# Retention attention and two feed-forward layers on one core: conversions begun in turn and kept in a PSUM bank, another order of the first loads

## The chip, the cores and the metric

One core of one Trainium2 chip. Time is device microseconds of one launch. The kernel before takes 644.09 us, the median of three runs (643.82 to 646.04).

## The reference

The inputs are q, k, v of shape (2, 8, 768, 64), one decay lam per head, and weights of two feed-forward layers. The weights are float64.

```
per block of 64 tokens, head by head (D[i,j] = lam^(i-j) for i >= j, else 0):
    out   = (q k^T * D) v + (q * lam^(i+1)) state
    state = lam^64 * state + (k * lam^(63-i))^T v
x = out as 1536 tokens x 512
h = x @ w_in                               # 512 x 2048
g = h where h >= 1, 0 where h <= -1, else (h + 1)^2 / 4
x = g @ w_out                              # 2048 x 512
y = ((x @ w_a) * (x @ w_b)) @ w2_out       # 512 x 1536 twice, 1536 x 512
```

## The kernel before, in words

**Attention.** The 1536 tokens are 12 chunks of 128 (6 per batch). `load_chunk` fetches four pieces of 256 KB per chunk (q and k by feature, k and v by token) into 16 buffers, named load. Per chunk, TensorE makes the scores (L149), VectorE multiplies them by the decay table dmask (`att_mask`, L179), GpSimd decays k (`att_kd`, L160) and q (`att_qd`, L171), TensorE sums the state's update (L193) and the output (L220 from the state, L224 from the masked scores). ScalarE casts the output to fp32r (the high part, L236), and VectorE subtracts that from it (the low part, L240). The three 512-token blocks of x hold high and low parts. The tables dmask and tabq are written to DRAM and read back by `tables`, which waits for GpSimd's powers of lam.

**Matrix products.** Each operand is a high and a low fp32r part, and a product is high x high + high x low + low x high: `mm3`, L354, three matmuls of 512 columns for each 128 of the inner dimension. `product_in` is 12 of them. A PSUM tile is one of eight banks, `bank()` hands them out in rotation.

**Weights.** `load_w` fetches one raw tile of 512 KB (128 x 512 float64) into one of four buffers, in the fixed order `order` of 68 tiles. `weight_pieces` is a generator that turns raw tiles into high and low parts, in pieces that `bg` takes between other work. Per tile: `begin` (ScalarE: absolute value of the upper word into hc, L279; the lower word scaled into c, L280), then VectorE clips hc (L292), shifts it into v (L294), joins the sign (L298) and adds c (L307); ScalarE casts the high part (`split_act`, L264), GpSimd subtracts (L265). `begin` of tile n+1 is issued inside tile n, after L298. `done(n)` runs the pieces until n tiles are ready. For the second layer, `strassen_weights` (L329) also forms sums and differences of a pair of tiles, s12 and s34, and splits them.

**Order.** Every engine works through its instructions in the order of the program, which is written out by hand. First the prologue (L514 to L575): tables, chunks 0 to 3, weight tiles 0 and 1, and fillers for TensorE (`warm`). Then the loop (L579 to L607): eight products of the first layer, `h_bank`, each beside the attention of one of the chunks 4 to 11. Then the stages of the first layer (L622 to L635). Then the second layer: six groups, each two calls of `both_banks` (a Strassen-like scheme over two token blocks, the third block by plain products) and three `o_stage`, which sum the output over the groups: in SBUF for blocks 0 and 1, in four banks held in PSUM for block 2 (`held`). All DMA of chunks and weights is issued by SP, in order; a `load_w` whose buffer is still being read holds up what is behind it.

Of the kernel before, what the change touches and what calls it, by code (L numbers as in the profile page):

```python
# [35 lines left out]
def retention_ffn_kernel(ctx: ExitStack, tc: tile.TileContext, lam, att, w1i, w1o, w2ab, w2o, out):  # L36
# [18 lines left out]
    four = deque(const.tile([128, 2, 512], F32R, name=f"four{i}") for i in range(19))  # L55
    two = deque(const.tile([128, 512], F32, name=f"two{i}") for i in range(18))

    banks = deque(ps_p.tile([128, 512], F32, name=f"ps{i}") for i in range(8))

    def bank():  # L60
        banks.rotate(-1)
# [4 lines left out]
    def t2(name):  # L66
        return two.popleft()

    def free2(*tiles):
        two.extend(tiles)  # L70
# [45 lines left out]
    def store_powers():  # L116
        nc.scalar.dma_start(out=raw_ap(CH + 1, [[PITCH, H], [8, 16], [1, 8]]), in_=base)
# [20 lines left out]
    def load_chunk(c, parts=(0, 1, 2, 3)):  # L138
        t = ck.setdefault(c, [None] * 4)
        for i in parts:  # L140
            t[i] = loads.popleft()
            nc.sync.dma_start(out=t[i], in_=att[c, i])
# [25 lines left out]
    def att_qd(c, engine):  # L168
        if c % CPB:
            qd[c] = t2("qd")  # L170
            engine.tensor_tensor(out=qd[c], in0=ck[c][0], in1=tabq.rearrange("p a i -> p (a i)"), op=ALU.mult)  # L171
        loads.append(ck[c][0])
# [83 lines left out]
    def load_w():  # L256
        if todo_loads:
            key = todo_loads.popleft()
            r = raw_p.tile([128, 1024], I32, tag="raw", name="raw")
            nc.sync.dma_start(out=r, in_=srcs[key[0]][key[1]].bitcast(I32))  # L260
            raws[key] = r
# [13 lines left out]
    def begin(key):  # L275

        r = raws[key].rearrange("p (c w) -> p c w", w=2)
        hc, c = t2("hc"), t2("c")
        nc.scalar.activation(out=hc, in_=r[:, :, 1].bitcast(F32), func=ACTF.Abs)  # L279
        nc.scalar.activation(out=c.bitcast(I32), in_=r[:, :, 0].bitcast(U32), func=ACTF.Copy, scale=2.0**-29)  # L280
        return hc, c

    def weight_pieces():

        nxt = begin(order[0])
        for n, key in enumerate(order):
            hc, c = nxt
            high = raws.pop(key).rearrange("p (c w) -> p c w", w=2)[:, :, 1]
            v = t2("v")


            nc.vector.tensor_scalar(out=hc, in0=hc, scalar1=HIGH_MIN, scalar2=HIGH_MAX, op0=ALU.max, op1=ALU.min)  # L292
            hc, v, c = (t.bitcast(I32) for t in (hc, v, c))
            nc.vector.tensor_scalar(  # L294
                out=v, in0=hc, scalar1=3, scalar2=0x3FFFFFFF, op0=ALU.logical_shift_left, op1=ALU.bitwise_and
            )
            yield 0
            nc.vector.scalar_tensor_tensor(  # L298
                out=v, in0=high, scalar=-0x40000000, in1=v, op0=ALU.bitwise_and, op1=ALU.bitwise_or
            )  # L300
            load_w()
            if n + 1 < len(order):
                if order[n + 1] not in raws:
                    load_w()
                nxt = begin(order[n + 1])
            yield 0
            nc.vector.tensor_tensor(out=v, in0=v, in1=c, op=ALU.add)  # L307
            hc, v, c = (t.bitcast(F32) for t in (hc, v, c))
            free2(hc, c)
            w = four.popleft()  # L310
            split_act(v, w[:, 0], w[:, 1])
            wt[key] = w
            if key[0] != "2i":
                free2(v)
            elif key[1] % 2 == 0:
                v_a.append(v)
            else:
                yield 0
                yield from strassen_weights(key[1] // 2, v_a.pop(), v)
            yield 1  # L320
# [88 lines left out]
    def both_banks(ft):  # L409

        wa, wb = wt["2i", 2 * ft], wt["2i", 2 * ft + 1]
        s12, s34 = sw.pop(ft)
        half_w = lambda w, i: [[w[:, a, (2 * i + j) * 128:(2 * i + j + 1) * 128] for a in range(2)] for j in range(2)]
        half_y = lambda nb, i: [[xy[nb][2 * i + j][:, a] for a in range(2)] for j in range(2)]
        half_t = lambda i: [[ts[i, j][:, a] for a in range(2)] for j in range(2)]

        def prod(w, x):
            ps = bank()
            mm3(ps, list(zip(w, x)))
            return ps  # L420

        add = lambda o, x, ps: nc.vector.tensor_tensor(out=o, in0=x, in1=ps, op=ALU.add)  # L422
        s, u, w, b0 = (t2(name) for name in ("s", "u", "w", "b0"))
        nc.scalar.copy(s, prod(half_w(wa, 0), half_y(0, 0)))  # L424
        bg()
        add(u, s, prod(half_w(s12, 1), half_t(2)))
        bg()
        a = t2("a")
        nc.scalar.copy(a, product_in("2i", 2 * ft, 2))
        bg(2)  # L430
        add(s, s, prod(half_w(wa, 1), half_y(0, 1)))
        add(w, u, prod(half_w(s34, 0), half_t(3)))
        bg()
        add(b0, w, prod(half_w(wb, 1), half_t(4)))
        nc.vector.tensor_tensor(out=b0, in0=b0, in1=s, op=ALU.mult)
        give_g(ft, 0, b0)
        pb = product_in("2i", 2 * ft + 1, 2)
        bg(2)
        nc.vector.tensor_tensor(out=a, in0=a, in1=pb, op=ALU.mult)
        give_g(ft, 2, a)  # L440
        pd = prod(half_w(s12, 0), half_t(1))
        add(w, w, pd)
        add(u, u, pd)
        add(u, u, prod(half_w(s34, 1), half_y(1, 1)))
        nc.vector.tensor_tensor(out=u, in0=u, in1=w, op=ALU.mult)
        give_g(ft, 1, u)
        free2(s, w)
        four.extend((s12, s34, wt.pop(("2i", 2 * ft)), wt.pop(("2i", 2 * ft + 1))))
# [34 lines left out]
    def o_bank(g, nb, m, last):  # L483
        fts = range(2 * g, 2 * g + 2)
        r0 = nb * TB + m * 128
        pairs = [([gt[2, f, nb][:, a, m * 128:(m + 1) * 128] for a in range(2)],
                  [wt["2o", f][:, b] for b in range(2)]) for f in fts]
        if nb < NB - 1:
            ps = bank()
            mm3(ps, pairs)  # L490
            o = acc["o", nb, m] = gather(acc.get(("o", nb, m)), ps, g == 0)
            if last:
                nc.sync.dma_start(out=out[r0:r0 + 128], in_=o)
            return
        mm3(held[m], pairs, g == 0, last)
        if last:
            o = t2("o")
            for i, copy, queue in ((0, nc.vector.tensor_copy, nc.sync), (1, nc.scalar.copy, nc.scalar)):
                cols = slice(i * DM // 2, (i + 1) * DM // 2)
                copy(o[:, cols], held[m][:, cols])  # L500
                queue.dma_start(out=out[r0:r0 + 128, cols], in_=o[:, cols])
# [13 lines left out]
    load_chunk(0, (0, 1))  # L515
    load_w()
    load_chunk(0, (2, 3))
    store_powers()
    tables()
    load_chunk(1)  # L520
    load_chunk(2)
    load_chunk(3)
    load_w()
    load_w()
    load_w()
    warm(8)
# [8 lines left out]
    bg(2)  # L535
    att_mask(0)
    low0 = att_out(0)
    att_scores(2)
    att_qd(0, nc.gpsimd)
    att_qd(1, nc.gpsimd)  # L540
    att_kd(1, nc.gpsimd)
    att_mask(1)
    low0()
    att_done(0)
    load_chunk(4, (0, 1, 2))
    add1 = att_state(1)
    add1()
    att_kd(2, nc.gpsimd)
    low1 = att_out(1)
    add2 = att_state(2)  # L550
    att_done(1)
    att_qd(2, nc.vector)
    att_scores(3)
    att_mask(2)
    low1()
    add2()
    att_kd(3, nc.gpsimd)
    low2 = att_out(2)
    att_done(2)
    att_qd(3, nc.gpsimd)  # L560
    add3 = att_state(3)
    att_mask(3)
    low2()
    add3()
    low3 = att_out(3)
    att_done(3)
    load_chunk(4, (3,))
    load_chunk(5)
    att_scores(4)
    bg()  # L570
    low3()
    att_kd(4, nc.gpsimd)
    att_qd(4, nc.gpsimd)
    att_mask(4)
    bg(2)  # L575


    at["limit"] = 8
    for nb in range(2):  # L579
        for j in range(4):  # L580
            c = 4 + 4 * nb + j
            low = []

            def attention():
                if j < 3 and c + 1 < NCHUNK:
                    att_scores(c + 1)

            h_bank(j, nb, attention)
            low = att_out(c)
            add = att_state(c)  # L590
            if j == 3 and c + 1 < NCHUNK:
                att_scores(c + 1)
            att_done(c)
            if c + 2 < NCHUNK:
                load_chunk(c + 2)
            if c + 1 < NCHUNK:
                if j < 3:
                    att_mask(c + 1)
                att_kd(c + 1, nc.gpsimd)
                att_qd(c + 1, nc.gpsimd)  # L600
            low()
            add()
            if j == 3 and c + 1 < NCHUNK:
                att_mask(c + 1)
            bg(3)
        if nb:
            done(8)  # L607
# [28 lines left out]


    groups = FF2 // 256
    for m in range(KT):
        held[m] = banks.popleft()  # L640
    for g in range(groups):
        at["limit"] = 32 + 6 * g + 6
# [58 lines left out]
```

## Time and profile before

| | |
|---|---|
| median of three runs | 644.09 us |
| the profiled execution | 646.91 us, its span 645.1 us |
| TensorE busy | 608.3 us (94%), granted clock 0.971 |
| VectorE busy | 489.1 us (76%) |
| ScalarE busy | 267.0 us (41%) |
| GpSimd busy | 282.4 us (44%) |
| DMA | 52.72 MB, mean 82 GB/s |

PE is TensorE, DVE is VectorE, ACT is ScalarE, POOL is GpSimd, SP issues DMAs. A row of the waits says who sat idle until whose instruction ended; L numbers are lines of the kernel above. The clock is the share of TensorE's full rate that was granted (1.00 is 2.4 GHz, 0.50 is 1.2 GHz). Times in windows and timelines count from the span's start.

### The profile page before, as it was taken

The numbers are of one execution on the slowest core, as the hardware profiler recorded it, in microseconds if no ns is written. First come the engines' busy times: TensorE is split into PE (matmuls) and PEld (weight loads), VectorE is DVE, ScalarE is ACT, GpSimd is POOL, SyncE is SP. The second block draws the span as 40 slices with busy tenths as digits, with TensorE's granted clock in tenths as the row PEclk, the third lists the DMA queues.
The fourth block names the chain that finished last, engine by engine and source line by source line (L and its number), as shares of the span: only waits on it lengthen the run. The fifth ranks groups of instructions, "written<-read, shape, count | busy, mean of one in ns | idle before, by whom it ended". The sixth has DMA issues, their size and how long they took to land. (4 is left out here: it accounts for less than half of the span.)

```text
span 645.1 us, 8349 instructions
## 1 busy us (share of the span) xinstructions
PE 608.3 (94%) x3099; PEld 496.0 (77%) x3100; DVE 489.1 (76%) x681; ACT 267.0 (41%) x473; POOL 282.4 (44%) x217
## 2 busy tenths in 40 slices
PE   6398889999999999999998999999989989989997
PEld 3386678888888888888886888878868878868886
DVE  2169863487775977597869999999969979969653
ACT  1135543366543544265545355534423433424210
POOL 2235662246433543343857455544533443444320
PEclk9689889999999999999999899999989999989999
DMA  5926560022110211022100222212202302300004
GB/s 163 359 90 222 197 198 2 33 99 98 66 66 34 99 65 66 33 90 67 41 1 34 65 99 66 98 33 99 99 0 70 102 26 69 105 23 2 1 17 179
DMA packets 21081, 52.72 MB, mean 82 GB/s; under 512 B 2600, under 2 KB 5168, under 8 KB 21040
## 3 DMA queue, kind: packets, MB, share of 16 engines
q1 hardware_dynamic: 19624, 51.39, 23.3%
q10 hardware_dynamic: 1416, 0.80, 0.5%
q8 instruction: 24, 0.39, 0.2%
q14 instruction: 17, 0.14, 0.1%
HBM read 49.03 MB, written 3.15 MB: 81 GB/s over the span
## 5 line engine op out<-in xcount | busy, mean ns | idle before, releaser
L265 POOL TENSOR_TENSOR four<-two,four 128x512 fp32r<-128x512 f32 x107 | 142.7, 1340 | 238.2 <-ACT four L264 214.0
L354 PE MATMUL ps<-block,four 128*128 128x512 f32 x828 | 200.8, 396 | 5.4 <-POOL block L265 2.3
L354 PEld LDWEIGHTS ps<-block,four 128*128 128x128 f32 x828 | 157.1, 191 | 40.8 <-POOL block L265 3.1
L354 PE MATMUL ps<-four,four 128*128 128x512 f32 x633 | 163.9, 393 | 4.1 <-ACT two L424 4.1
L354 PEld LDWEIGHTS ps<-four,four 128*128 128x128 f32 x633 | 119.6, 189 | 30.7 <-ACT two L424 5.3
L264 ACT CAST four<-two 128x512 fp32r<-128x512 f32 x107 | 66.0, 620 | 137.7 <-DVE two L307 42.9
L265 POOL TENSOR_TENSOR late_four<-two,late_four 128x512 fp32r<-128x512 f32 x46 | 62.6, 1363 | 58.0 <-ACT late_four L264 42.6
L354 PE MATMUL ps<-block,late_four 128*128 128x512 f32 x324 | 77.2, 389 | 0.0
L354 PEld LDWEIGHTS ps<-block,late_four 128*128 128x128 f32 x324 | 60.8, 188 | 12.6
L354 PE MATMUL ps<-four,late_four 128*128 128x512 f32 x243 | 64.9, 393 | 2.0 <-ACT late_two L424 2.0
L354 PE MATMUL ps<-late_four,four 128*128 128x512 f32 x213 | 59.9, 396 | 0.1
L373 ACT ACTIVATE two<-two,half 128x512 f32<-128x512 f32 x42 | 30.4, 723 | 66.1 <-DVE two L372 66.1
L422 DVE TENSOR_TENSOR two<-two,ps 128x512 f32<-128x512 f32 x66 | 44.1, 683 | 15.6 <-PE ps L354 9.6
L372 DVE TENSOR_SCALAR two<-ps 128x512 f32<-128x512 f32 x42 | 28.8, 686 | 35.6 <-PE ps L354 35.5
L354 PEld LDWEIGHTS ps<-four,late_four 128*128 128x128 f32 x243 | 45.9, 189 | 11.9 <-ACT late_two L424 2.4
L458 DVE TENSOR_TENSOR two<-two,ps 128x512 f32<-128x512 f32 x60 | 40.4, 678 | 18.6 <-PE ps L354 18.6
L298 DVE SCALAR_TENSOR_TENSOR two<-raw,two 128x512 int32<-128x512 int32 x56 | 53.1, 949 | 0.4
L264 ACT CAST late_four<-two 128x512 fp32r<-128x512 f32 x46 | 28.5, 622 | 55.6 <-DVE two L307 13.5
L354 PEld LDWEIGHTS ps<-late_four,four 128*128 128x128 f32 x213 | 40.8, 192 | 9.1 <-DVE two L422 0.6
L307 DVE CUSTOM_DVE_ANT_0 two<-two,two 128x1024 uint16<-128x1024 uint16 x51 | 46.1, 905 | 1.8
L279 ACT ACTIVATE two<-raw 128x512 f32<-128x512 f32 x55 | 36.8, 670 | 12.9 <-DMA raw<-in_w1i 12.9
L292 DVE TENSOR_SCALAR two<-two 128x512 f32<-128x512 f32 x55 | 33.3, 606 | 11.5 <-ACT two L279 11.5
(103 smaller groups left out, 649.8 us busy)
## 6 DMA issues: line engine op xcount, KB each, us to landing
load<-in_att SPq DMA_DIRECT2D x48, 256.0 KB, 5.0
raw<-in_w2ab SPq DMA_DIRECT2D x24, 512.0 KB, 3.2
raw<-in_w1i SPq DMA_DIRECT2D x16, 512.0 KB, 3.3
raw<-in_w1o SPq DMA_DIRECT2D x16, 512.0 KB, 3.3
raw<-in_w2o SPq DMA_DIRECT2D x12, 512.0 KB, 3.2
out<-two SPq DMA_DIRECT2D x6, 256.0 KB, 2.0
dmask<-rows SPq DMA_DIRECT2D x2, 256.0 KB, 4.6
out<-late_two SPq DMA_DIRECT2D x2, 256.0 KB, 2.0
```

The source lines that it names most:

```text
L264: nc.scalar.copy(hi, src)
L265: (engine or nc.gpsimd).tensor_tensor(out=lo, in0=src, in1=hi.bitcast(F32), op=ALU.subtract)
L279: nc.scalar.activation(out=hc, in_=r[:, :, 1].bitcast(F32), func=ACTF.Abs)
L292: nc.vector.tensor_scalar(out=hc, in0=hc, scalar1=HIGH_MIN, scalar2=HIGH_MAX, op0=ALU.max, op1=ALU.min)
L298: nc.vector.scalar_tensor_tensor(out=v, in0=high, scalar=-0x40000000, in1=v, op0=ALU.bitwise_and, op1=ALU.bitwise_or)
L307: nc.vector.tensor_tensor(out=v, in0=v, in1=c, op=ALU.add)
L354: nc.tensor.matmul(out=ps, lhsT=l[a], rhs=r[b], start=(start and i == 0 and j == 0), stop=(stop and i == n - 1 and j == 2))
L372: nc.vector.tensor_scalar(out=r, in0=ps, scalar1=-1.0, scalar2=1.0, op0=ALU.max, op1=ALU.min)
L373: nc.scalar.activation(out=r, in_=r, func=ACTF.Square, scale=0.5, bias=half)
L422: add = lambda o, x, ps: nc.vector.tensor_tensor(out=o, in0=x, in1=ps, op=ALU.add)
L458: nc.vector.tensor_tensor(out=total, in0=total, in1=ps, op=ALU.add)
```

## The change

- `begin` of tile n is issued at the head of tile n for tiles 0 to 3, and inside tile n-1 only from tile 4 on.
- The absolute value goes to one PSUM bank of its own, `words`, in place of an SBUF buffer; clip and shift stay there, and L298 reads it. Seven banks rotate in place of eight.
- In the prologue, q and k of chunk 1 are loaded ahead of the tables, weight tile 1 ahead of chunk 3, and chunks 4 to 6 are loaded before the loop, which then fetches chunk c + 3 in place of c + 2. Scores of chunks 2 and 3 are issued after the output of the chunk before. The pieces of tile 1 are spread over chunks 2 to 4.
- In `both_banks` the last sums of a and b stay in the bank of their product (pf, pg), and the product a x b reads them there.
- Of block 2's output, the first 128 rows (m = 0) are no longer held in PSUM but summed in SBUF as those of the other blocks.

```diff
-    banks = deque(ps_p.tile([128, 512], F32, name=f"ps{i}") for i in range(8))
+    banks = deque(ps_p.tile([128, 512], F32, name=f"ps{i}") for i in range(7))
+    words = ps_p.tile([128, 512], F32, name="words")
...
-        hc, c = t2("hc"), t2("c")
-        nc.scalar.activation(out=hc, in_=r[:, :, 1].bitcast(F32), func=ACTF.Abs)
+        c = t2("c")
+        nc.scalar.activation(out=words, in_=r[:, :, 1].bitcast(F32), func=ACTF.Abs)
...
-        nxt = begin(order[0])
+        nxt = None
         for n, key in enumerate(order):
-            hc, c = nxt
+            c = nxt or begin(key)
+            nxt = None
...
-            nc.vector.tensor_scalar(out=hc, in0=hc, scalar1=HIGH_MIN, scalar2=HIGH_MAX, op0=ALU.max, op1=ALU.min)
-            hc, v, c = (t.bitcast(I32) for t in (hc, v, c))
             nc.vector.tensor_scalar(
-                out=v, in0=hc, scalar1=3, scalar2=0x3FFFFFFF, op0=ALU.logical_shift_left, op1=ALU.bitwise_and
+                out=words, in0=words, scalar1=HIGH_MIN, scalar2=HIGH_MAX, op0=ALU.max, op1=ALU.min
+            )
+            word, v, c = (t.bitcast(I32) for t in (words, v, c))
+            nc.vector.tensor_scalar(
+                out=word, in0=word, scalar1=3, scalar2=0x3FFFFFFF, op0=ALU.logical_shift_left, op1=ALU.bitwise_and
             )
             yield 0
             nc.vector.scalar_tensor_tensor(
-                out=v, in0=high, scalar=-0x40000000, in1=v, op0=ALU.bitwise_and, op1=ALU.bitwise_or
+                out=v, in0=high, scalar=-0x40000000, in1=word, op0=ALU.bitwise_and, op1=ALU.bitwise_or
             )
             load_w()
-            if n + 1 < len(order):
+            if 4 <= n + 1 < len(order):
...
-        add(b0, w, prod(half_w(wb, 1), half_t(4)))
-        nc.vector.tensor_tensor(out=b0, in0=b0, in1=s, op=ALU.mult)
+        pf = prod(half_w(wb, 1), half_t(4))
+        add(pf, w, pf)
+        nc.vector.tensor_tensor(out=b0, in0=s, in1=pf, op=ALU.mult)
...
-        add(u, u, prod(half_w(s34, 1), half_y(1, 1)))
-        nc.vector.tensor_tensor(out=u, in0=u, in1=w, op=ALU.mult)
+        pg = prod(half_w(s34, 1), half_y(1, 1))
+        add(pg, u, pg)
+        nc.vector.tensor_tensor(out=u, in0=w, in1=pg, op=ALU.mult)
...
-        if nb < NB - 1:
+        if m not in held or nb < NB - 1:
...
     load_chunk(0, (2, 3))
+    load_chunk(1, (0, 1))
     store_powers()
     tables()
-    load_chunk(1)
+    load_chunk(1, (2, 3))
     load_chunk(2)
+    load_w()
     load_chunk(3)
-    load_w()
     load_w()
     load_w()
...
     low0 = att_out(0)
-    att_scores(2)
     att_qd(0, nc.gpsimd)
+    att_kd(1, nc.gpsimd)
     att_qd(1, nc.gpsimd)
-    att_kd(1, nc.gpsimd)
     att_mask(1)
     low0()
     att_done(0)
-    load_chunk(4, (0, 1, 2))
     add1 = att_state(1)
     add1()
+    low1 = att_out(1)
+    att_done(1)
+    att_scores(2)
     att_kd(2, nc.gpsimd)
-    low1 = att_out(1)
+    att_qd(2, nc.gpsimd)
+    low1()
+    att_mask(2)
     add2 = att_state(2)
-    att_done(1)
-    att_qd(2, nc.vector)
-    att_scores(3)
-    att_mask(2)
-    low1()
     add2()
-    att_kd(3, nc.gpsimd)
     low2 = att_out(2)
     att_done(2)
+    bg(1)
+    load_chunk(4)
+    att_scores(3)
+    low2()
+    att_kd(3, nc.gpsimd)
     att_qd(3, nc.gpsimd)
+    att_mask(3)
     add3 = att_state(3)
-    att_mask(3)
-    low2()
     add3()
     low3 = att_out(3)
     att_done(3)
-    load_chunk(4, (3,))
     load_chunk(5)
+    bg(1)
+    low3()
     att_scores(4)
-    bg()
-    low3()
     att_kd(4, nc.gpsimd)
     att_qd(4, nc.gpsimd)
+    bg(1)
     att_mask(4)
-    bg(2)
+    load_chunk(6)
...
-            if c + 2 < NCHUNK:
-                load_chunk(c + 2)
+            if c + 3 < NCHUNK:
+                load_chunk(c + 3)
...
-    for m in range(KT):
+    for m in range(1, KT):
         held[m] = banks.popleft()
```

## Rows read from the trace of the kernel before

**Rows 1.** Windows by stage: length, busy and count per engine, clock, DMA share, GB/s.
```profile
0.00:44.50 44.50, 28.83 (x275) 20.81 (x276) 13.41 (x30) 9.97 (x24) 14.16 (x17) 0.81 0.63 219
44.50:107.20 62.70, 54.97 (x547) 44.51 (x545) 48.88 (x71) 30.44 (x64) 31.73 (x25) 0.92 0.47 160
107.20:345.00 237.80, 237.80 (x1051) 196.98 (x1050) 178.97 (x236) 113.28 (x188) 108.37 (x79) 1.00 0.17 58
345.00:575.00 230.00, 220.32 (x941) 179.06 (x940) 205.44 (x283) 97.14 (x170) 108.61 (x82) 0.98 0.21 69
```

**Rows 2.** Waits of TensorE over the span: us in total, times, longest.
```profile
PE ps L149 <- DMA load<-in_att: 10.5, 4, 3.2
PE ps L193 <- POOL two L160: 8.7, 1, 8.7
PE ps L354 <- ACT two L424: 4.1, 3, 1.9
PE ps L354 <- POOL block L265: 2.3, 2, 1.9
PE ps L354 <- ACT late_two L424: 2.0, 1, 2.0
```

**Rows 3.** Window behind the wait at 470.
```profile
470.80:474.10 3.30, 3.30 (x10) 2.53 (x9) 1.42 (x3) 0.00 (x0) 0.20 (x1) 0.50 0.00 0
```

**Rows 4.** Timeline of the front: start, us, engine, instruction, in brackets idle before it.
```profile
11.05 8.44 SPq L142 DMA_DIRECT2D load<-in_att  x12
...
13.47 0.43 DVE L292 TENSOR_SCALAR two<-two 128x512 f32<-128x512 f32 x1 [11.49 <-ACT two L279]
...
15.83 1.28 DVE L179 TENSOR_TENSOR two<-ps,dmask 128x512 f32<-128x512 f32 x2
...
17.92 2.08 PE L149 MATMUL ps<-load,load 64*128 64x128 f32 x16 [3.16 <-DMA load<-in_att]
...
27.16 0.66 ACT L279 ACTIVATE two<-raw 128x512 f32<-128x512 f32 x1 [12.89 <-DMA raw<-in_w1i]
...
28.95 1.27 POOL L265 TENSOR_TENSOR four<-two,four 128x512 fp32r<-128x512 f32 x1 [18.55 <-ACT four L264]
...
31.39 3.05 POOL L160 TENSOR_TENSOR two<-load,kdf 128x512 f32<-128x512 f32 x3
...
32.49 1.12 PE L193 MATMUL ps<-load,two 128*64 128x64 f32 x16 [8.66 <-POOL two L160]
...
44.54 3.18 PE L354 MATMUL ps<-block,four 128*128 128x512 f32 x12
```

**Rows 5.** VectorE's lines 294 and 372: ns min/median/max, first and last start.
```profile
L294 DVE TENSOR_SCALAR two<-two x45: 426/430/1458, 13.9 to 598.3; 128x512 int32<-128x512 int32 x45
...
L372 DVE TENSOR_SCALAR two<-ps x42: 676/691/693, 47.8 to 325.1; 128x512 f32<-128x512 f32 x42
```

**Rows 6.** Timeline of TensorE at the end of the loop.
```profile
95.59 3.01 PE L354 MATMUL ps<-block,four 128*128 128x512 f32 x12
...
102.13 3.06 PE L354 MATMUL ps<-block,four 128*128 128x512 f32 x12
...
107.16 1.19 PE L354 MATMUL ps<-four,four 128*128 128x512 f32 x4
```

**Rows 7.** VectorE's lines in the loop, 44.5 to 107.2: count, busy, mean ns, idle before.
```profile
L298 DVE SCALAR_TENSOR_TENSOR two<-raw,two 128x512 int32<-128x512 int32 x7 | 7.8, 1108 | 0.1
...
L307 DVE CUSTOM_DVE_ANT_0 two<-two,two 128x1024 uint16<-128x1024 uint16 x7 | 5.2, 742 | 0.1
L294 DVE TENSOR_SCALAR two<-two 128x512 int32<-128x512 int32 x6 | 5.1, 853 | 0.3
L292 DVE TENSOR_SCALAR two<-two 128x512 f32<-128x512 f32 x6 | 4.7, 787 | 0.0
```

**Rows 8.** Timeline of VectorE ahead of the wait at 470.
```profile
456.71 1.57 DVE L445 TENSOR_TENSOR two<-two,two 128x512 f32<-128x512 f32 x1
...
462.59 1.73 DVE L298 SCALAR_TENSOR_TENSOR two<-raw,two 128x512 int32<-128x512 int32 x1
...
465.64 3.29 DVE L329 TENSOR_TENSOR two<-two,two 128x256 f32<-128x256 f32 x3
```

More of the change, by code (lines that the diff above doesn't have):

```diff
@@ L277, in begin @@
         r = raws[key].rearrange("p (c w) -> p c w", w=2)
-        hc, c = t2("hc"), t2("c")
-        nc.scalar.activation(out=hc, in_=r[:, :, 1].bitcast(F32), func=ACTF.Abs)
+        c = t2("c")
+        nc.scalar.activation(out=words, in_=r[:, :, 1].bitcast(F32), func=ACTF.Abs)
         nc.scalar.activation(out=c.bitcast(I32), in_=r[:, :, 0].bitcast(U32), func=ACTF.Copy, scale=2.0**-29)
-        return hc, c
+        return c
     def weight_pieces():
-        nxt = begin(order[0])
+        nxt = None
         for n, key in enumerate(order):
-            hc, c = nxt
+            c = nxt or begin(key)
+            nxt = None
             high = raws.pop(key).rearrange("p (c w) -> p c w", w=2)[:, :, 1]
             v = t2("v")
-            nc.vector.tensor_scalar(out=hc, in0=hc, scalar1=HIGH_MIN, scalar2=HIGH_MAX, op0=ALU.max, op1=ALU.min)
-            hc, v, c = (t.bitcast(I32) for t in (hc, v, c))
             nc.vector.tensor_scalar(
-                out=v, in0=hc, scalar1=3, scalar2=0x3FFFFFFF, op0=ALU.logical_shift_left, op1=ALU.bitwise_and
+                out=words, in0=words, scalar1=HIGH_MIN, scalar2=HIGH_MAX, op0=ALU.max, op1=ALU.min
[3 more added lines that the diff above has]
+                out=word, in0=word, scalar1=3, scalar2=0x3FFFFFFF, op0=ALU.logical_shift_left, op1=ALU.bitwise_and
             )
@@ L307, in weight_pieces @@
             nc.vector.tensor_tensor(out=v, in0=v, in1=c, op=ALU.add)
-            hc, v, c = (t.bitcast(F32) for t in (hc, v, c))
-            free2(hc, c)
+            v, c = (t.bitcast(F32) for t in (v, c))
+            free2(c)
             w = four.popleft()
```

## The prediction

> **What bounds the kernel now.** I read the windows by stage first, then TensorE's waits, then the timelines around them. From 107.2 to 345 us TensorE is busy in all 237.8 us at the full clock (2.4 GHz) and starts 1051 matmuls: 0.226 us each [rows 1]. Nothing that only relieves another engine can shorten that stretch. What can be won lies in three places. **Front**, 0 to 44.5: TensorE is busy for 28.8 us, part of it fillers, at a clock of 0.81. **Loop**, 44.5 to 107.2 (attention of chunks 4 to 11 between the first eight products): 55.0 us busy, clock 0.92. **Second layer**, 345 to 575: 941 matmuls x 0.226 = 212.9 us of work in 230 us, so 17 us are lost [rows 1]. The largest waits are on DMA for chunks (10.5), on GpSimd for decayed keys (8.7, one wait), and on ScalarE's copy L424 (4.1 + 2.0) [rows 2]. The list of waits doesn't hold the price of the lower clock: after 470.8 us TensorE, which had stood idle for 1.96 us, is granted 0.50 (1.2 GHz): 10 matmuls reach into 3.3 us, of which I count 8 whole ones, 0.41 each, so 8 x (0.41 - 0.226) = 1.5 us are lost without any wait in the list [rows 3].
>
> The front's wait has its cause far from where it shows. ScalarE sits idle for 12.89 us until raw weight tile 1 lands at 27.16, since the conversion of tile 1 was begun inside that of tile 0. Behind it stand ScalarE's cast of tile 0 and the first attention output; GpSimd waits 18.55 us for that cast, so the keys of chunk 1 (L160) are decayed from 31.4 on, and TensorE resumes at 32.49 [rows 4].
>
> **Part by part: the front.** `begin` of tiles 1 to 3 now comes in turn, so nothing of tile 1 stands in ScalarE's queue until three chunks' attention has been issued. Tile 0's conversion then runs through: VectorE starts it at 13.47 [rows 4], and three steps of 0.69 (a VectorE step reading PSUM, L372) [rows 5], the add, 0.69, the cast, 0.66 like the abs, and the low part, 1.27 [rows 4], end at 18.2. GpSimd follows with kd(1), 1.02 (3.05 for three) [rows 4]: 19.3. That is what TensorE waits for at 32.49. From there to the first 512-column product took 12.05 us, 32.49 to 44.54 [rows 4], a part of it at half clock. The same work now includes scores(2), 1.2 to 2.0 us: 19.3 + 12.05 + 2 = 33.4.
>
> What is late next: scores(2) and scores(3) are no longer issued a chunk ahead, so the two masks (1.28 us a pair) [rows 4] stand between scores and output. 1.3 to 2 us idle for each of two chunks: 36 to 37. SP's queue: q and k of chunk 1 now go ahead of the tables, so scores(1), which waited 3.16 us until 17.92 [rows 4], runs at 14.8, behind the fillers. The two transfers (0.7 us each: twelve are issued in 8.44) [rows 4] may push the tables 0 to 1.3 us back, and the mask at 15.83 with them. Tile 1, 0.5 MB, is moved before chunk 3: 1.3 us later for chunk 3, which is needed after 24: tile 1 landed at 27.16 behind all of chunk 3 [rows 4], so by then chunk 3 is there in either order. I take 36.5: **8.0 us won**, bounds 33.4 (11.1) and 40 (4.5, if the pauses hold the clock at half).
>
> **The loop.** Chunks are fetched three ahead instead of two, behind the same waits of SP, so a whole iteration (6.5 us, 95.59 to 102.13) [rows 6] earlier. The two waits for chunks in this stretch (3.0 and 1.7 of the 10.5) go, and most of the half clock behind them. The chunk buffers suffice: 16 hold four chunks, and the new one takes the place of the one before the last. What then bounds it is VectorE. An iteration gives it a clip, a maximum, two masks, a low part and half a state add, 3.8 us by steps of 0.68 to 0.69, plus four thirds of a conversion. That now costs 0.79 + 0.85 + 1.11 + 0.74 = 3.49 [rows 7], so 8.5 us against 6.5 of TensorE. With the words in PSUM it is 3 x 0.69 + 0.74 = 2.81, so 7.6. The conversions end after four and a half iterations: 4.5 x 7.6 + 2.5 x 6.5 + 5.0 (last one, 102.13 to 107.16) [rows 6] = 55.5; I add 0.5 for tiles 2 and 3, whose abs now follows the square on ScalarE while VectorE waits. 56.0 against 62.6: **6.6 us won**. Bounds: 50.8 (7 x 6.54 + 5.0; 11.8 won) and 60 (2.6).
>
> **The words in PSUM.** The trace holds both sides. A step that reads and writes SBUF (L294) has a minimum of 0.43 and a maximum of 1.46; one that reads PSUM (L372) stays within 0.676 and 0.693 over 42 instances [rows 5]. So the change gives up the 0.43 of a free moment and gives up the long ones, which fall where GpSimd works. The VectorE page of the Trainium skill (VectorE: DVE Perf Modes, Why PSUM operands drop a tier) speaks against it: a PSUM operand takes an fp32 single-source step from two results a cycle to one. The minima agree (0.43 against 0.68). By that rule alone clip and shift lose 0.25 each per tile, and it is a rival below. ScalarE's abs into PSUM has no row here; into SBUF it took 0.66 [rows 4]. I take the same, with half and twice of it as bounds: both leave ScalarE under half busy in 107.2 to 345, where it stands at 113 of 238 us [rows 1], and move no term.
>
> An added wait: there is one bank of words, so the abs of tile n+1 waits until VectorE's third step of tile n has read it. Behind it on ScalarE stands the copy c (about as long as the abs) and the cast of tile n: 0.6 us later than now. On VectorE the add, 0.69, covers the abs. In 107.2 to 345 a product's parts are wanted a stage later, and ScalarE has that idle time, so I cost it at nothing; without that cover 0.6 us x 34 tiles = 20 us.
>
> **The second layer.** Its stalls are one pattern, four times: VectorE's backlog holds back ScalarE's cast of s34, behind that stands L424, and TensorE has no free bank. Around 470: L445 took 1.57, the third step of each tile about 1.7 (1.73 shown), three L329 3.29 [rows 8]. New: L445 0.69 (-0.9); per tile two steps +0.25 and one -1.0 (-0.5, twice). Against it: m = 0 is no longer held in PSUM, which puts one add of 0.68 into just this queue (six in all, none on another path), and the wait for abs, some 0.1. Sum -1.1 against 1.96 of waiting; L329 still meets GpSimd and can take 0.4 more or 0.9 less. Remaining 0.8, which I take as too short to cost the clock. So 1.2 per stall, and 1.5 more at two of the four (470 and 568), which the half clock followed: 1.2 + 2.7 + 1.2 + 2.7 = 7.8; at 351 to 355, where TensorE waits for GpSimd's low parts (2.3) [rows 2], I take 0.1, as that queue is full by itself: **7.9 us won** of 17. Bounds: 2 and 14. Banks: 7 rotate in place of 8 before 345, 4 as now afterwards (8 - 1 - 3); pf and pg keep theirs one step, 0.69, longer, and are wanted again four products later. The end stays.
>
> **Sum.** 8.0 + 6.6 + 7.9 = 22.5. The profiled execution took 646.9 (645.1 span and 1.8 around it), so 624.4; the median of the runs is 2.8 lower, and I forecast 644.1 - 22.5 = 621.6.
>
> **Rivals.** (a) Only the front is won: in the loop and the second layer VectorE's saving goes into its own backlog. 644.1 - 8 - 2.6 - 2 = 631.5. For it: VectorE is busy in 205 of 230 us of the second layer [rows 1]. Against: the waits hang on 1.7 us steps that disappear. 0.18.
> (b) All goes: 644.1 - 11 - 11 - 14 = 608. For it: after 1 us less backlog a stall of 1.96 may vanish and the clock with it. 0.12.
> (c) Reading PSUM costs and frees nothing: the third step stays long for another reason than its second SBUF operand, and clip and shift cost 0.25 each more. Then each of the four stalls grows by four such steps and the add of m = 0, 1.7 in all, some 7 us: 644.1 - 14.6 + 7 = 636.5. Against: L372 never exceeds 0.693. 0.06. (This is what the rule of the Trainium skill named above, VectorE: DVE Perf Modes, Why PSUM operands drop a tier, gives if it is taken alone.)
> (d) Slower: the single bank couples ScalarE and VectorE in the second layer. In each of the twelve calls of `both_banks` L424 then leaves behind abs 0.66, c 0.66 and the new add 0.68, 2.0 us later, and each pause brings 1.5 us of half clock: 12 x 3.5 = 42, so 644.1 - 14.6 + 42 = 671.5. It decides from 14.6 / 12 = 1.2 us a call. Against: seven of the twelve calls have no wait now. 0.06.
> (e) The front doesn't move, because the tables and chunk 1 set it (mask at 15.83 and data until 24) and the pauses keep the clock at half: 644, with the rest given back. 0.03.
> The forecast, 613 to 628, has 0.55. Range 608 to 632.5: it leaves out a third of (b) and all of (c), (d), (e), 0.19. A measurement of this kernel tells 0.5%, 3.2 us, from no change. Faster: 0.55 + 0.18 + 0.12 + two thirds of (c) = 0.89; same 0.04; slower 0.07.
>
> **What will show it.** Right: the first 512-column product at 35 to 38; no wait of ScalarE on a weight's DMA; no wait for chunks after 40; L292, L294, L298 within 0.65 to 0.72; the loop's end at 90 to 95; L424 waits under 3 us in sum; no wait in the 238 us that follow the loop. Wrong: a first product after 40; new waits there; TensorE waiting on banks in more calls than four.

## The result, and the profile after

The changed kernel takes 619.0 us, the kernel before 643.96 (medians of four runs each); the ratio is 0.962, interval 0.9567 to 0.9673. 621.6 had been forecast, range 608 to 632.5. The profiled execution took 620.1, its span 618.3. So 26.8 us of span are to be accounted for. By the medians it is 25.0, as the profiled execution of the kernel before lay 2.9 us above its median (646.91), and that of the kernel after 1.1.

The windows by stage of the kernel after, with its own borders: front, loop, rest of the first layer, and 230 us of the second layer.
```profile
0.00:36.60 36.60, 28.06 (x276) 19.09 (x276) 14.09 (x30) 9.73 (x23) 15.04 (x18) 0.91 0.76 267
36.60:95.44 58.84, 51.85 (x547) 41.65 (x545) 44.30 (x70) 30.70 (x64) 31.18 (x25) 0.97 0.49 170
95.44:333.20 237.76, 237.76 (x1051) 196.94 (x1050) 166.02 (x236) 112.98 (x188) 104.95 (x79) 1.00 0.17 58
333.20:563.20 230.00, 228.56 (x1007) 188.47 (x1006) 202.84 (x307) 103.79 (x179) 113.28 (x87) 1.00 0.21 69
```
Against [rows 1]: the front ends 7.9 us sooner, the loop is 3.8 us shorter, the 1051 matmuls behind it take the same 237.8 us, and 230 us of the second layer hold 1007 matmuls in place of 941, with a clock of 1.00 in place of 0.98. The loop's end, at 95.4, lies just behind the 90 to 95 that were to show the forecast right.

TensorE's waits after, to be read against [rows 2].
```profile
PE ps L221 <- POOL two L172: 5.5, 2, 4.6
PE ps L225 <- DVE two L180: 4.0, 4, 2.5
PE ps L150 <- DMA load<-in_att: 2.5, 1, 2.5
PE ps L194 <- POOL two L161: 2.2, 2, 1.5
PE ps L358 <- POOL block L266: 1.4, 1, 1.4
PE ps L115 <- DVE idle L98: 1.2, 1, 1.2
```
The waits on the copy of the first product of a call of `both_banks` (L424 before, L428 now) are gone altogether, and of those on chunks only the very first is left. New are two in the loop for GpSimd, 4.6 us for the decayed q (L172) and 1.5 for the decayed keys (L161), and four on the masks in the front (L225), 4.0 in sum.

The front's timeline after, to be read against [rows 4].
```profile
14.57 0.70 DVE L294 TENSOR_SCALAR words<-words 128x512 f32<-128x512 f32 x1 [12.60 <-ACT words L280]
...
18.29 1.28 POOL L266 TENSOR_TENSOR four<-two,four 128x512 fp32r<-128x512 f32 x1 [7.95 <-ACT four L265]
...
19.52 1.05 POOL L161 TENSOR_TENSOR two<-load,kdf 128x512 f32<-128x512 f32 x1
...
20.61 1.12 PE L194 MATMUL ps<-load,two 128*64 128x64 f32 x16 [0.72 <-POOL two L161]
...
30.56 0.64 ACT L280 ACTIVATE words<-raw 128x512 f32<-128x512 f32 x1
...
36.61 3.17 PE L358 MATMUL ps<-block,four 128*128 128x512 f32 x12
```
GpSimd waits 7.95 us for the cast of tile 0, not 18.55. TensorE resumes at 20.6, not 32.5, and ScalarE's begin of tile 1 stands at 30.56, without any wait for its DMA.

VectorE in the second layer ahead of what was the wait at 470, to be read against [rows 8]; the matmul that waited there starts at 451.24 now.
```profile
440.57 0.68 DVE L464 TENSOR_TENSOR two<-two,ps 128x512 f32<-128x512 f32 x1
441.17 0.69 DVE L294 TENSOR_SCALAR words<-words 128x512 f32<-128x512 f32 x1
441.89 0.70 DVE L298 TENSOR_SCALAR words<-words 128x512 int32<-128x512 int32 x1
442.68 0.69 DVE L302 SCALAR_TENSOR_TENSOR two<-raw,words 128x512 int32<-128x512 int32 x1
443.51 0.69 DVE L311 CUSTOM_DVE_ANT_0 two<-two,two 128x1024 uint16<-128x1024 uint16 x1
444.12 0.69 DVE L294 TENSOR_SCALAR words<-words 128x512 f32<-128x512 f32 x1
444.84 0.70 DVE L298 TENSOR_SCALAR words<-words 128x512 int32<-128x512 int32 x1
445.63 0.69 DVE L302 SCALAR_TENSOR_TENSOR two<-raw,words 128x512 int32<-128x512 int32 x1
446.46 0.69 DVE L311 CUSTOM_DVE_ANT_0 two<-two,two 128x1024 uint16<-128x1024 uint16 x1
447.25 0.42 DVE L333 TENSOR_TENSOR two<-two 128x256 f32<-128x256 f32 x1
447.71 2.19 DVE L333 TENSOR_TENSOR two<-two,two 128x256 f32<-128x256 f32 x3
```
The first line is the new add. Two tiles and their sums take 8.7 us (441.17 to 449.90); before, from 458.20 to 468.93, 10.7. Every step of a tile is 0.69 to 0.70 here, where one was 1.7 before.

### The profile page after: what moved, and what is told of

It is laid out like the page before. It is cut to its first block, busy times and chain, and to the rows that moved or that the text cites. A ratio compares the mean times of both kernels' runs of the same rounds, so it can differ in the third digit from the quotient of the medians.

```text
span 618.3 us, 8380 instructions
## 1 busy us (share of the span) xinstructions
PE 597.7 (97%) x3100; PEld 488.4 (79%) x3100; DVE 457.3 (74%) x684; ACT 267.8 (43%) x473; POOL 278.5 (45%) x218
## 4 chain that ended last, share of the span: by engine, by line
PE 82%; DVE 8%; ACT 4%; POOL 2%; issue 2%; DMA 1%; ACTq 0%; DVEq 0%; POOLq 0%
PE ps L358 79%; DVE words L294 1%; PE ps L225 1%; PE ps L221 1%; DVE two L302 1%; DVE words L298 1%; DVE two L401 1%; DMA lamp<-in_lam 1%; ACT words L280 1%; DVE two L311 1%; PE ps L150 1%; DVE two L180 1%; DMA rows<-base 1%; ACT four L265 1%; ACT two L281 0%
## 5 line engine op out<-in xcount | busy, mean ns | idle before, releaser
L358 PE MATMUL ps<-block,four 128*128 128x512 f32 x828 | 196.9, 391 | 1.4 <-POOL block L266 1.4
L358 PEld LDWEIGHTS ps<-block,four 128*128 128x128 f32 x828 | 154.6, 188 | 35.4 <-POOL block L266 1.8
L358 PE MATMUL ps<-four,four 128*128 128x512 f32 x633 | 162.0, 389 | 0.0
L280 ACT ACTIVATE words<-raw 128x512 f32<-128x512 f32 x68 | 43.1, 634 | 55.0 <-DVE two L302 49.7
L294 DVE TENSOR_SCALAR words<-words 128x512 f32<-128x512 f32 x68 | 47.0, 691 | 17.4 <-ACT words L280 17.4
L358 PE MATMUL ps<-late_four,four 128*128 128x512 f32 x213 | 58.5, 389 | 0.0
L464 DVE TENSOR_TENSOR two<-two,ps 128x512 f32<-128x512 f32 x62 | 42.2, 680 | 13.1 <-PE ps L358 13.1
L311 DVE CUSTOM_DVE_ANT_0 two<-two,two 128x1024 uint16<-128x1024 uint16 x54 | 49.7, 921 | 1.9
L298 DVE TENSOR_SCALAR words<-words 128x512 int32<-128x512 int32 x68 | 47.5, 699 | 2.3
L426 DVE TENSOR_TENSOR two<-two,ps 128x512 f32<-128x512 f32 x50 | 32.9, 682 | 19.2 <-PE ps L358 16.7
```

The source lines that it names most:

```text
L280: nc.scalar.activation(out=words, in_=r[:, :, 1].bitcast(F32), func=ACTF.Abs)
L294: nc.vector.tensor_scalar(out=words, in0=words, scalar1=HIGH_MIN, scalar2=HIGH_MAX, op0=ALU.max, op1=ALU.min)
L298: nc.vector.tensor_scalar(out=word, in0=word, scalar1=3, scalar2=0x3FFFFFFF, op0=ALU.logical_shift_left, op1=ALU.bitwise_and)
L358: nc.tensor.matmul(out=ps, lhsT=l[a], rhs=r[b], start=(start and i == 0 and j == 0), stop=(stop and i == n - 1 and j == 2))
L464: nc.vector.tensor_tensor(out=total, in0=total, in1=ps, op=ALU.add)
```

## The experiments

Each is timed beside the kernel before on the same chip; the chip is not the same for all of them. The stages come from the timelines: start of the first 512-column matmul, of the 97th (the loop's end), of the 1153rd (first of the second layer), and the end of the last.

| kernel | median us | before beside it | first product | loop | second layer |
|---|---|---|---|---|---|
| before | 643.96 | | 44.5 | 62.6 | 294.7 |
| after | 619.0 | 643.96 | 36.6 | 58.8 | 279.7 |
| front alone | 635.16 | 643.3 | 33.7 | 61.2 | 292.3 |
| words in SBUF | 630.52 | 643.3 | 35.5 | 61.2 | 290.0 |
| sums in SBUF | 621.79 | 643.3 | 35.5 | 59.5 | 281.8 |
| PSUM alone | 626.28 | 643.3 | 44.1 | 56.5 | 279.7 |
| decay first | 617.47 | 644.71 | 34.4 | 58.4 | 279.8 |
| two banks of words | 621.16 | 644.71 | 36.6 | 58.5 | 283.5 |
| chunks two ahead | 620.56 | 644.71 | 35.3 | 59.5 | 279.8 |
| tiles 1 to 3 begun ahead | 621.89 | 644.71 | 40.0 | 57.3 | 279.7 |
| fewer pieces | 615.73 | 644.61 | 34.6 | 57.8 | 280.1 |
| fewer pieces, decay first | 615.3 | 644.61 | 35.4 | 55.2 | 279.7 |
| third step alone | 618.84 | 644.61 | 34.1 | 58.6 | 282.8 |
| only tile 1 in turn, on top of fewer pieces, decay first | 611.32 | 642.97 | 35.9 | 51.1 | 280.1 |

The first layer between loop and second layer takes 239.50 us in all fourteen. One profile stands for each kernel: with one and the same prologue the first product varies from 34.4 to 36.6, so a difference of 2 us there is nothing. A profiled execution can also lie some us from the median of its kernel: 2.9 below it for front alone (632.24), 2.3 above it for two banks of words (623.48), 1.6 above it for fewer pieces (617.32) and for third step alone (620.41). A difference of a microsecond or two between two loops is therefore weak evidence; the second layer, without stalls, repeats within 0.4 us.

**Front alone.** The kernel before with the prologue and loads of after, and:
```diff
-            hc, c = nxt
+            hc, c = nxt or begin(key)
+            nxt = None
...
-            if n + 1 < len(order):
+            if 4 <= n + 1 < len(order):
...
-                load_chunk(c + 2)
+                load_chunk(c + 3)
```


> The kernel before with the new order of the front alone (loads, prologue, chunks three ahead, conversions of tiles 1 to 3 begun in turn); words in SBUF, sums of a and b in SBUF, eight banks, all four sums of block 2 held. Theory A (the three gains are separate, and the second layer's comes from VectorE's steps that no longer meet GpSimd): first 512-column product at 36 to 38, loop 59 to 62 us long, second layer with its stalls as before, so 631 to 635 us. Rival B (the second layer's stalls went because the work before it is laid differently in time): its stalls are gone here too, 619 to 623 us.

635.16 (ratio 0.9865, 0.983 to 0.9901): theory A, with the time 0.2 above its range and the first product, 33.7, ahead of its 36 to 38. The second layer's waits on L425 (L424 in the kernel before) are 6.3 us in sum, against 6.1 before, so rival B is out.

**Words in SBUF.** The changed kernel with the `hc` buffer and the v of before in the three steps.
```diff
-        nc.scalar.activation(out=words, in_=r[:, :, 1].bitcast(F32), func=ACTF.Abs)
+        nc.scalar.activation(out=hc, in_=r[:, :, 1].bitcast(F32), func=ACTF.Abs)
```


> The changed kernel with the words back in SBUF buffers; seven banks still rotate (the eighth lies unused), the rest as changed. Theory A, words first (of the 15.0 us won behind the first layer most is owed to the conversions' three steps): L298's mean returns to 0.95 to 1.1 us, the stalls of the second layer return by more than half, loop 1 to 3 us longer: 627 to 632 us. Rival A', sums first (it is L445, 0.9 us in front of each stall): 619 to 622 us. Rival C (the single bank's wait costs more than PSUM saves): under 617 us.

630.52 (0.98, 0.9771 to 0.983): words first. Its waits, and the shift and third step (L296, L300 in this kernel; ns min/median/max):
```profile
PE ps L356 <- ACT two L426: 5.0, 3, 1.7
```
```profile
L296 DVE TENSOR_SCALAR two<-two x48: 426/430/1565, 15.1 to 583.2; 128x512 int32<-128x512 int32 x48
```
```profile
L300 DVE SCALAR_TENSOR_TENSOR two<-raw,two x58: 677/692/1801, 15.5 to 584.7; 128x512 int32<-128x512 int32 x58
```
Three waits of up to 1.7 are back, on the same copy. The medians are better than with PSUM (the shift, 0.43 against 0.70) or close to it (the third step, 692 ns against 679). It is the long ones, up to 1.8 us, that return.

**Sums in SBUF.**
```diff
-        pf = prod(half_w(wb, 1), half_t(4))
-        add(pf, w, pf)
-        nc.vector.tensor_tensor(out=b0, in0=s, in1=pf, op=ALU.mult)
+        add(b0, w, prod(half_w(wb, 1), half_t(4)))
+        nc.vector.tensor_tensor(out=b0, in0=b0, in1=s, op=ALU.mult)
```
and the same for u.

> The changed kernel with the last sums of a and b back in SBUF, the rest as changed. Theory A, words first: L445's line costs 1.1 us in the mean again, a pause under 1 us returns before some of the second calls of a group: 619 to 623 us. Rival A', sums first: the four stalls return, 627 to 632 us.

621.79 (0.9655, 0.9635 to 0.9674): words first again. The product with both operands in SBUF took 1.07 us in the mean (nine of them), and one wait of 0.8 came back. So the second layer goes from 294.7 (292.3 in the front-alone profile) to 290.0 by the sums, to 281.8 by the words, to 279.7 by both.

**PSUM alone.** The changed kernel with the old prologue, `load_chunk(c + 2)` and `if n + 1 < len(order)`.

> The changed kernel with the front of before (prologue, loads two ahead, tile 1 begun inside tile 0); words and sums in PSUM as changed. Theory A: first product at 44 to 46, the second layer free of stalls, the loop 60 to 63 us: 627 to 630 us. Rival B: stalls in the second layer as before, 638 to 645 us. Together with the front alone, theory A has the two gains add up to that of the whole change within 3 us.

626.28 (0.9735, 0.9716 to 0.9753): theory A in the second layer, which is to the hundredth as in after. The front is worth 8.1 by itself and PSUM 17.0, in sum 25.1; the whole change 25.0. The loop was not as expected: 56.5 in place of 60 to 63, with 3.7 us of waits for chunks in it, and the time is 0.7 below the range. It takes 58.8 after, so by these two profiles the new front gives 2.3 of its gain back in the loop.

**Decay first.**
```diff
+            if c + 1 < NCHUNK:
+                att_kd(c + 1, nc.gpsimd)
+                att_qd(c + 1, nc.gpsimd)
             h_bank(j, nb, attention)
```
(and not behind the product any more).

> The changed kernel with the decays of the next chunk's k and q put ahead of the product of the same iteration in the loop, so that they stand before that product's low part in GpSimd's queue. Theory P (the loop's remaining wait, 4.62 us for the decayed q of chunk 7, comes from the place in GpSimd's queue, behind a low part that waits for VectorE and ScalarE): the waits on L172 in the loop fall under 1 us, the loop takes 52 to 55 us in place of 58.8, time 612 to 616 us. Rival V (VectorE's backlog sets the loop's pace wherever the decay stands): the wait moves to the masks or to ScalarE's cast, loop 57 to 59 us, 618 to 621 us.

617.47 (0.9582, 0.955 to 0.9615), loop 58.4: rival V in the loop; the time lies between the ranges of P and V, and its interval overlaps that of after. The wait on L172 is gone, and others have taken its place:
```profile
PE ps L358 <- ACT block L237: 3.2, 1, 3.2
PE ps L150 <- DMA load<-in_att: 2.6, 1, 2.6
PE ps L221 <- POOL four L266: 1.6, 1, 1.6
```
The product now waits 3.2 us for ScalarE's cast of the attention output.

**Two banks of words.**
```diff
+        words.reverse()
+        return words[1], c
...
-    for m in range(1, KT):
+    for m in range(2, KT):
```
(words is a list of two banks, six others rotate, and `warm` writes into the second bank of words).

> The changed kernel with two banks of words in turn, so that the abs of tile n+1 no longer waits for the third step of tile n; to pay for it six banks rotate, two sums of block 2 are held in place of three, and TensorE's fillers write into the second bank of words. Theory W (the added wait costs in the loop: there abs and copy stand ahead of the square): loop 56 to 58 us, second layer as changed (279.7 us from its first product to TensorE's end), 616.5 to 618.5 us. Rival N (the wait is covered): loop 58 to 60 us, 618.5 to 621 us; with four banks for the second layer as before and one more add per group no loss there.

621.16 (0.9645, 0.9609 to 0.9681): neither. The loop is unchanged (58.5), so N holds there; but the second layer loses 3.8 us, against both. Its three waits of up to 1.1 on the copy L430 suggest how little room after has: the second sum that is not held puts one more add of 0.68 per group in VectorE's queue and takes one more rotating bank. Which of the two it is was not tried, and the profiled execution is the longest of the four.

**Chunks two ahead.** `load_chunk(c + 2)`, and chunk 6 not before the loop.

> The changed kernel with chunks loaded two ahead as before (chunk 6 not before the loop). Theory D (three ahead took away the waits for chunks): one or two waits on DMA of 2 to 3 us return in the loop, loop 60 to 63 us, 621 to 625 us. Rival V (the loop is held by VectorE's backlog, and the chunk would be waited for beside it): loop 58 to 60 us, 618.5 to 620.5 us.

620.56 (0.9627, 0.9593 to 0.966): theory D on the waits (8.6 us on DMA in sum, one of 4.3 and one of 1.8 in the loop), rival V on the loop and, within 0.1, on the time: the loop grew by 0.7 only, as TensorE no longer waited for GpSimd instead. By itself the third chunk ahead is worth nothing that can be told here.

**Tiles 1 to 3 begun ahead.**
```diff
-            if 4 <= n + 1 < len(order):
+            if n + 1 < len(order):
```


> The changed kernel with tiles 1 to 3 begun inside the tile before, as all others; loads and prologue as changed. Theory T (the front's gain is ScalarE no longer waiting for raw tile 1): tile 1 lands at about 23 us now, ScalarE stands still until then with the cast of tile 0 behind it, first product at 39 to 42, 622 to 626 us. Rival L (the loads' order alone does it): first product at 36 to 38, and with tiles 2 and 3 begun earlier a loop of 56 to 58 us, 616 to 619 us.

621.89 (0.9649, 0.9611 to 0.9688): theory T for the front and, within 0.1, for the time, and the half of rival L that I had not given T: a shorter loop, 57.3. ScalarE's wait is back, only shorter because tile 1 is loaded sooner:
```profile
22.95 0.62 ACT L280 ACTIVATE words<-raw 128x512 f32<-128x512 f32 x1 [7.55 <-DMA raw<-in_w1i]
```
First product 40.0. So beginning tile 1 in turn is worth 3.4 us against after, and up to 5.6 against the earliest first product with that prologue (34.4). Beginning tiles 2 and 3 in turn seems to cost 1.5 in the loop.

**Fewer pieces.** The loop of after holds this, of an iteration whose product had ended at 52.4 (engines' timeline, chosen lines).
```profile
57.42 0.68 DVE L376 TENSOR_SCALAR two<-ps 128x512 f32<-128x512 f32 x1
57.54 0.64 ACT L280 ACTIVATE words<-raw 128x512 f32<-128x512 f32 x1 [1.50 <-DVE two L302]
...
58.68 0.71 ACT L377 ACTIVATE two<-two,half 128x512 f32<-128x512 f32 x1
...
62.43 1.04 POOL L161 TENSOR_TENSOR two<-load,kdf 128x512 f32<-128x512 f32 x1
...
63.43 1.29 POOL L172 TENSOR_TENSOR two<-load,tabq 128x512 f32<-128x512 f32 x1
...
64.77 1.97 PE L221 MATMUL ps<-two,st 64*64 64x128 f32 x16 [4.62 <-POOL two L172]
```
VectorE comes to the clip 5 us late; behind it follow, one after the other, square, maximum, cast, low part, decays, and TensorE. So VectorE gets less to do at the end of each iteration:
```diff
-            bg(3)
+            bg(2)
```


> The changed kernel with two pieces of conversion in place of three at the end of each iteration of the loop, so three with that inside the product: tiles 2 to 7 are spread over six iterations and not four and a half. Theory V (in the loop VectorE's backlog sets the pace: 3.8 us of attention and product and 4/3 x 2.9 of conversion against 6.5 of TensorE): VectorE's load falls to 6.7 us an iteration, the wait for the decayed q of chunk 7 falls under 1.5 us, loop 54 to 56 us, 614 to 617 us. Rival G (it is GpSimd's queue, its low parts and decays): loop 57.5 to 59 us, 618.5 to 620.5 us.

615.73 (0.9556, 0.9528 to 0.9584): the time of theory V, but a loop of 57.8 and still a wait of 2.6 for L172, which is G's. The profile is of the longest of six executions, 617.32, where three took 614.3 to 614.5; how long the loop was in those is not known, so V and G are not told apart by it.

**Fewer pieces, decay first.** Both edits.

> As the run with two pieces, and the decays of the next chunk ahead of the product as well. Theory V: the backlog is the cause and the place in the queue adds little: within 1.5 us of the run with two pieces alone. Rival VG (both hold the loop, each hides the other): loop 51 to 53.5 us, 611 to 613.5 us.

615.3 (0.9548, 0.9523 to 0.9573), loop 55.2: in time within 0.5 us of fewer pieces, as V has it; in the loop 2.6 shorter by the two profiles, and longer than VG's 51 to 53.5. The time is the better evidence, as fewer pieces was profiled in its longest execution.

**Third step alone.**
```diff
-        nc.scalar.activation(out=words, in_=r[:, :, 1].bitcast(F32), func=ACTF.Abs)
+        nc.scalar.activation(out=hc, in_=r[:, :, 1].bitcast(F32), func=ACTF.Abs)
...
-                out=words, in0=words, scalar1=HIGH_MIN, scalar2=HIGH_MAX, op0=ALU.max, op1=ALU.min
+                out=hc, in0=hc, scalar1=HIGH_MIN, scalar2=HIGH_MAX, op0=ALU.max, op1=ALU.min
...
-                out=word, in0=word, scalar1=3, scalar2=0x3FFFFFFF, op0=ALU.logical_shift_left, op1=ALU.bitwise_and
+                out=word, in0=ic, scalar1=3, scalar2=0x3FFFFFFF, op0=ALU.logical_shift_left, op1=ALU.bitwise_and
```


> The changed kernel with abs and clip in SBUF buffers and only the shift's result in the PSUM bank, so that the third step (the join of the sign, L302) reads one operand from SBUF and one from PSUM, and the abs no longer waits for the bank. Theory J (what the words in PSUM won is the third step, which has two SBUF operands otherwise): L302 stays at 0.68 us, clip at 0.42 in free moments and up to 1.5 beside GpSimd; second layer 279.7 to 282 us, 616 to 621 us. Rival K (each of the three steps counts, clip and shift too): stalls of 0.5 us or more return at second calls, second layer 283 to 288 us, 622 to 627 us.

618.84 (0.9614, 0.9587 to 0.9641), second layer 282.8: J's time, and a second layer between J's 279.7 to 282 and K's 283 to 288. VectorE's three steps in this kernel, ns min/median/max:
```profile
L294 DVE TENSOR_SCALAR two<-two x57: 411/421/1516, 14.7 to 569.9; 128x512 f32<-128x512 f32 x57
```
```profile
L298 DVE TENSOR_SCALAR words<-two x57: 694/695/696, 15.1 to 570.4; 128x512 int32<-128x512 int32 x57
```
```profile
L302 DVE SCALAR_TENSOR_TENSOR two<-raw,words x58: 676/680/690, 15.9 to 572.2; 128x512 int32<-128x512 int32 x58
```
Three waits of up to 0.2 return on the copy, where words in SBUF had three of up to 1.7. So of the 10.3 us that the words bring in the second layer (290.0 to 279.7), 7.2 come with shift and third step, 3.1 with abs and clip.

**Only tile 1 in turn**, on top of fewer pieces, decay first.
```diff
-            if 4 <= n + 1 < len(order):
+            if 2 <= n + 1 < len(order):
```


> As the run with two pieces and the decays first, and tiles 2 and 3 begun inside the tile before them, so that only tile 1 is begun in turn. Theory S (in the loop's first two iterations VectorE waits 1.3 us for an abs that stands behind the square on ScalarE): these waits go, first product at 34 to 37 as before, loop 53 to 54.5 us in place of 55.2, 613 to 615 us. Rival: the abs, ahead of the casts of the prologue now, holds these back, first product at 37 to 39 and 616 to 618 us.

611.32 (0.9502, 0.9477 to 0.9527), loop 51.1: theory S in its sign, more than twice its size. This version beats both kernels: by the ratios to the kernel before it stands at 0.950 against 0.962, clear of each other's intervals, and by the medians, which were not taken side by side, 7.7 us under after. In its loop two waits of 0.8 and 0.2 are left, and no half clock.

## Why the prediction was right, step by step

**First layer behind the loop: nothing to win.** Right: 237.8 us and 1051 matmuls in both, no wait there.

**Front, 8.0 forecast, 7.9 measured.** Right, with its mechanism: with tiles begun ahead again ScalarE's wait is back and 3.4 us of the gain gone; the rest is tile 1 being loaded sooner and the order of the prologue, which were not separated. That it agrees to 0.1 is luck: the first product varies by 2 us from profile to profile. Inside, the decayed keys of chunk 1 were ready 1.3 us later than I had (20.6, not 19.3), because the tables were pushed back by 1.1, as the text had allowed, and ScalarE's abs and VectorE's start (14.57, not 13.47) with them; the two pauses at the masks were 0.2 and 1.3 in place of 1.3 to 2 each. These cancel.

**Loop, 6.6 forecast, 3.8 measured.** The mechanism was right in that VectorE sets the pace: with PSUM alone the loop takes 56.5, with the front alone 61.2, and before 62.6. The waits for chunks mattered less than the text gives to understand: with chunks two ahead 6.1 us of them are back in the loop, and it is 0.7 longer. Two terms were mis-sized. The first is "I add 0.5 for tiles 2 and 3": beginning them in turn cost 1.5 by the run with tiles begun ahead (loop 58.8 to 57.3), and 4.1 once the other two delays were gone (55.2 to 51.1). The second is that I counted VectorE's load and not the chain behind it. From a late clip six steps on three engines follow before TensorE gets its q. By the medians decay first and fewer pieces bring 1.5 and 3.3 us against after, both together 3.7, and with the third 7.7. So the place of the decays adds next to nothing to fewer pieces. The loops, 0.5, 1.0, 3.7 and 7.8 shorter, look as if the delays hid each other, but each is of one profile, that of fewer pieces of its longest execution. How the three share it is thus not settled. My floor of 50.8 was within reach: 51.1.

**Words in PSUM.** Right. The steps of after:
```profile
L294 DVE TENSOR_SCALAR words<-words x68: 681/690/700, 14.6 to 570.2; 128x512 f32<-128x512 f32 x68
```
```profile
L298 DVE TENSOR_SCALAR words<-words x68: 698/699/700, 15.3 to 570.9; 128x512 int32<-128x512 int32 x68
```
```profile
L302 DVE SCALAR_TENSOR_TENSOR two<-raw,words x62: 676/679/689, 16.0 to 572.7; 128x512 int32<-128x512 int32 x62
```
No long one is left among them, where [rows 5] had 1458 ns. That GpSimd is what they met shows in the traces: all 31 of the 68 third steps that took over 0.72 us before ran beside a GpSimd instruction; after, 43 of 68 run beside one, and none is long. The rule that spoke against the change (the Trainium skill, VectorE: DVE Perf Modes, Why PSUM operands drop a tier) is true of the minima, 0.41 to 0.68. It is outweighed: with abs and clip in SBUF, the clip at a median of 0.42, the second layer is 3.1 us longer. What decides is stated in the Trainium skill (SBUF — State Buffer, Who interferes with whom): a VectorE instruction with one SBUF input at most, outside the two-port modes, does not contend with GpSimd; one with two contends with a GpSimd instruction that reads SBUF. The trace agrees: the third step ran from 677 to 1801 ns with two SBUF inputs, and from 676 to 690 with one. The add behind it (L311) still reads two, and 20 of its 68 instances after took 1.40 us in the mean, all of them beside GpSimd.

**The added wait.** It is there: ScalarE stands idle for 55.0 us in 30 waits of the abs on L302. It costs TensorE nothing that I could find: with two banks of words the loop is 0.3 shorter, and in the second layer after TensorE has one wait, of 1.4, on another engine. Rival (d) had its wait, and not its price.

**Second layer, 7.9 forecast, 15.0 measured.** The step that failed is "Remaining 0.8": nothing remained. From the start of the product (456.71 at L445 before, 439.96 at L451 now) to the end of the last L333, 12.2 us became 9.9, so 2.3 went where I had 1.1 and the wait was 1.96. The product gave 0.9, the tiles' steps 0.9, and the new add took 0.6, all near the forecast. The three L333 (L329 before) gave 1.1, which the sum had at nothing and at best 0.9. They met GpSimd less, as its low part came later: the cast ahead of it now starts 0.35 us behind the add L311, held up by abs and copy, where it started 0.04 behind it. Over all 48 instances they took 0.94 us in the mean before, 0.95 with words in SBUF and 0.86 after. With the pauses the half clock went at all places. The four stalls, not quite alike (1.4 us of waiting at 420 to 424, 1.95 to 1.96 at the others), gave 1.7, 3.8, 2.2 and 3.9 us, by the shift between the same matmuls of both traces (15.04 to 16.77, 16.76 to 20.60, 20.60 to 22.84, 22.86 to 26.72), 11.7 in sum against 7.8. At the fifth place, 351 to 355, where I had 0.1, 3.0 came: GpSimd's queue was not full by itself, its wait fell from 2.3 to 1.4, and the half clock behind it went. With words in SBUF that wait is 2.3 again, with sums in SBUF 1.4, so it is the words. Rival (b), which has all of it go, was nearest here.

So 4.3 us of span were won beyond the forecast (2.5 by the medians): I had 7.1 too little in the second layer and 2.8 too much in the loop. That the total came within 2.6 us of the forecast owes something to these two misses of opposite sign.

## What to carry to other kernels

Where VectorE and GpSimd both work on SBUF, look at the spread of an instruction's durations, not at its minimum: a spare PSUM bank for an intermediate value costs 0.26 us a step with one input here, nothing for one with two, and takes away delays of 1.0. Before a load is moved, look which engine's queue stands still for it: here the cure was to take the dependent instruction out of ScalarE's queue and only then to load sooner. And when a stretch is held by several delays in a row, taking one away moves the wait to the next: with the decays first TensorE no longer waited 4.6 us for the decayed q, but 3.2 for ScalarE's cast, and the time did not move beyond its noise; three edits together brought 7.7.

## What the runs showed that I had not expected

For the shift it is enough to write PSUM: reading SBUF and writing PSUM it took 694 to 696 ns, and 52 of its 68 instances ran beside a GpSimd instruction. ScalarE's abs was quicker into PSUM than into SBUF, 638 ns against 669 (medians). The Trainium skill's tip on destinations (ScalarE: Activation LUTs, Step-by-step: what each stage is for) has this in direction; nothing in the time hangs on these 31 ns. And the length of a pause alone does not tell whether the clock falls: in the kernel before, TensorE stood idle for 1.96 us at 470, 1.95 at 520 and 1.95 at 568; half clock (0.50) followed the first and the third, full clock (1.00) the second.
